# A convolution and SwiGLU kernel on one core: activation fetch in 1024-byte packets, eight sums on VectorE, the first output in column tiles, the last stores on two queues

## The chip, the cores and the metric

The kernel runs on one core of a Trainium2 chip. The metric is device time in microseconds of one execution. The engines are TensorE (PE; its weight loads are PEld), VectorE (DVE), ScalarE (ACT), GpSimd (POOL) and SyncE (SP), which issues most DMAs. ScalarE issues some.

## The reference

A causal convolution over time with 7 taps for each of 8 heads (taps are a softmax), then RMS norm and a feed-forward layer with SwiGLU. 8 x 4096 tokens of 192 features, 1536 hidden features, all in float32:

```python
w = softmax(weight, axis=-1)                       # 8 heads x 7 taps
attn = einsum('hk,bskhg->bshg', w, unfold(x))      # causal, 24 features a head
x = attn.reshape(32768, 192)
xn = x / sqrt(mean(x * x, axis=-1) + 1e-6) * rms_g
g, val = xn @ w_gate, xn @ w_val                   # 192 -> 1536
out = (g * sigmoid(g) * val) @ w_out               # 1536 -> 192
```

## The kernel before

The 32768 tokens are worked in 32 pairs of 1024 tokens (two groups g of 512). Gate and value weights stand side by side on the partitions: of each tile of 128 partitions the lower 64 rows belong to the gate, the upper 64 to the value, and a feature's 192 inputs are three slices k of 64 rows. So a product is six matmuls: three slices, each in two row halves that run beside each other.

**Pair 0** (`plain`, L1073) multiplies plainly. Its hidden values `ht` are multiplied with `wo_sb` in `outer` (L1098 on; matmuls L1114): 128 tokens as weights, 192 features as moving columns, the hidden features in two row halves. ScalarE copies the lower half's sums out of PSUM (L1122), VectorE adds the upper half's (L1126), and two stores of 384 KB go out (L1131).

**Pair 1** (word list `FIRST`) multiplies its products plainly too (L874), but its output already goes the way of all later pairs: `step` (L926) issues six matmuls that use 32 columns of the array each, with 32 features of the weights as stationary tile and 384, 256 or 128 columns of tokens. Between the products ten combinations of the weights are prepared for all later pairs. `prepare` splits each into three parts: a difference on GpSimd for some (L752), high bits on VectorE (L755), a scaled copy on ScalarE (L759), the rest on VectorE (L761), a difference on GpSimd (L765), a last copy on ScalarE (L767) and a store to DRAM (`wd`, L771). Two buffers take turns, so weight n waits until weight n - 2 is stored. The word `W` in the list is one such step.

**Pairs 2 to 31** (word list `ORDER`, once in each window `w`) use seven-product schemes on both levels: the products (L902) take split operands, float32 in three parts, from a ring of ten slots that is loaded from `wd` (L788); sums of hidden values (`h_sum`, L953) and of output accumulators (L970, L1000) make good for the products saved. `split` (L670, L816, L818) and `x_sum` (L830) make the operands' parts for the next pair while the present one runs.

The words name the engine, the act and the chunk: `Gh1.0` is h sum 1 of chunk 0 on GpSimd, `Vh1.0` the same on VectorE; `Aga.0` a silu on ScalarE (L976), `Vma.0` the product of silu and value (L983), which frees a PSUM bank; `p1` the next product or step on PE; `+` and `-` point to the next pair and the one before. A word's place in the list is its place in its engine's own order, and nothing else: each engine works its instructions in that order and waits where an operand isn't there.

A pair's activations are convolved in a layout of their own, stored to DRAM (`xd`, L1036, 192 rows of 4096 bytes), and fetched with features on the partitions in six transfers of 64 rows (`fetch`, L634). The tile that takes them is `xb`, for pair 2 `lent`, which lies where the ring will be. The first cast of a window (`An.0`, L670 on ScalarE) waits for the fetch of one slice. The next pairs' inputs are loaded by `load_head` (L149).

A pair's output is transposed on VectorE in blocks of 32 (`turn`, L941) and leaves in five stores for each of the two groups (`leave`, L1025). `leave` chooses the queue: `q = nc.scalar if c > 0 and p == PAIRS - 1 else queue(eng)`.

Of the kernel before, what the change touches and what calls it, by code (L numbers as in the profile page):

```python
# [20 lines left out]
def kernel(  # L21
# [10 lines left out]
    nc = tc.nc  # L32
# [34 lines left out]
    NP = FC // 2  # L67
    SPAN = 1509
# [168 lines left out]
    lent = spc.tile([P, 2 * KP * T], F32, name="ring")  # L237
# [107 lines left out]
    rb = cst.tile([P, KP, 2, T], F32, name="xb")  # L345
    lent4 = lent[:].rearrange("p (k g t) -> p k g t", k=KP, g=2)
# [3 lines left out]
    xb = rb[:].rearrange("p k g t -> p g k t")  # L350
# [297 lines left out]

    def pick(h, full):

        i = next((i for i in free[h] if ((h, i) in whole) == full), free[h][0])
        free[h].remove(i)
        return i

# [149 lines left out]

    def operand(g, p):
        if g < KP:
            return tokens(p)[:, g]
        return tt[:, 0:2, :] if g == 3 else tt[:, 2:4, :]

    def split(act, g, eng, p):  # L810
        src, high = operand(g, p), split_of(g, 0)
        e = engine.get(eng)
        if act == "n":
            copy(eng, high.bitcast(F32R), src)
        elif act == "l":
            e.tensor_tensor(out=split_of(g, 1).bitcast(F32R), in0=src, in1=high, op=ALU.subtract)  # L816
        else:
            nc.vector.scalar_tensor_tensor(  # L818
                out=split_of(g, 2).bitcast(F32R), in0=high, scalar=1.0 + SPLIT, in1=src,
                op0=ALU.mult, op1=ALU.subtract,  # L820
            )

    def x_sum(i, eng, p):
        a11, a21, a12, a22, e1, e2 = (tokens(p)[:, k // 2, k % 2] for k in range(6))
        s1, s2, s4, s3 = (tt[:, k, :] for k in range(4))
# [8 lines left out]
    class Pair:  # L834
        def __init__(self, p):
            self.p = p
            self.bk, self.o_sb, self.sg = {}, {}, {}
            self.open_half = {}
            self.line = self.products()
# [27 lines left out]
        def products(self):  # L867
            if self.p == 1:
                for j, c in PLAIN:
                    g, f = CELL[c]  # L870
                    self.open((j, c), False)
                    for k in range(KP):
                        for h in range(2):
                            nc.tensor.matmul(  # L874
                                out=self.both(j, c)[:, h, :], lhsT=wf[HALF[h], k, 2 * j + f, :],
                                rhs=rb[HALF[h], k, g, :], start=(k == 0), stop=(k == KP - 1),
# [33 lines left out]
        def step(self, form, k):  # L910
# [5 lines left out]
            right = RIGHT[form][:, k]  # L916
            two = src.rearrange("p (b q e) -> p q b e", q=2, e=Q)
            for i in range(2):
                self.tile(b, i, 0, WIDE, right[:, i], src[:, 0:WIDE], fresh)
            for i in range(2):  # L920
                self.tile(b, 2 + i, 0, T // 2, right[:, 2], two[:, i], fresh)
            for i in range(2):
                self.tile(b, 2 + i, T // 2, T - WIDE, right[:, i], src[:, WIDE:T], False)
# [31 lines left out]
        def do(self, eng, name):  # L955
# [47 lines left out]
            elif act in ("T22", "T21"):  # L1003
                self.turn(tt[:, 7 if act == "T22" else 8, :], 1, int(act[2]) - 1)
            elif act in ("T11", "T12"):
# [3 lines left out]
            else:  # L1009
                self.leave(int(act[2]), j, eng)  # L1010

        def leave(self, g, i, eng):
# [11 lines left out]
            q = nc.scalar if c > 0 and p == PAIRS - 1 else queue(eng)  # L1024
            q.dma_start(out=to, in_=o[i * Q : i * Q + n, lo:hi, :])  # L1025
# [75 lines left out]
    LAG = 138  # L1101

    STEP = 100 * D / T
    OUT = 2 * (T // P) * FC * STEP
    OVER = 50

    def outer(p, hts, base):


        def mm(h, bks, g, j, w, f, first, give=None):  # L1110
            if first:
                bks[h] = free[h].pop(0) if first is True else pick(h, False)
                whole.discard((h, bks[h]))
            nc.tensor.matmul(  # L1114
                out=bank(h, bks[h])[:, w : w + D],
                lhsT=hts[f // NF][HALF[h], g, f % NF, j * P : (j + 1) * P],
                rhs=wo_sb[HALF[h], f, :], start=(f == 0 and w == 0),
                stop=(f == FC - 1), skip_group_check=True,
            )

        def low(dst, bks, n):
            nc.scalar.copy(out=dst, in_=bank(0, bks[0])[:, 0:n])  # L1122
            free[0].append(bks[0])

        def upp(dst, bks, n):
            nc.vector.tensor_tensor(out=dst, in0=bank(1, bks[1])[:, 0:n], in1=dst, op=ALU.add)  # L1126
            free[1].append(bks[1])

        def store(g, o_sb, lo=0, hi=T // P):
            r = p * PT + g * T  # L1130
            nc.sync.dma_start(  # L1131
                out=out[r + lo * P : r + hi * P, :].rearrange("(j p) d -> p j d", p=P),
                in_=o_sb[:, lo:hi, :],
            )

        def soon(*a):
            put(base + n * STEP + LAG + OVER + 1, functools.partial(store, *a))

        n = 0

        def mms(bks, g, j, w, fs, first):
            nonlocal n
            for i, f in enumerate(fs):
                for h in range(2):
                    at = base + n * STEP + h * LAG
                    put(at, functools.partial(mm, h, bks, g, j, w, f, first if i == 0 else False))
                n += 1

        def evac(dst, bks, w):
            put(base + n * STEP + OVER, functools.partial(low, dst, bks, w))  # L1150
            put(base + n * STEP + LAG + OVER, functools.partial(upp, dst, bks, w))

        for g in range(2):
            o_sb = outs.tile([P, T // P, D], F32, name="o_sb")
            if g == 0:

                bks = [{}, {}]
                for fs in (range(0, FC // 2), range(FC // 2, FC - NF)):
                    for j in range(4):
                        mms(bks[j // 2], g, j, j % 2 * D, fs, j % 2 == 0 and fs[0] == 0)  # L1160
                for j in range(4):
                    mms(bks[j // 2], g, j, j % 2 * D, range(FC - NF, FC), False)
                    if j % 2:
                        dst = o_sb[:, j - 1 : j + 1, :].rearrange("p j d -> p (j d)")
                        evac(dst, bks[j // 2], 2 * D)
            else:
                for j in range(0, 2 if p == PAIRS - 1 else 4, 2):
                    b = {}
                    mms(b, g, j, 0, range(FC), "used" if j else True)
                    mms(b, g, j + 1, D, range(FC), False)  # L1170
                    evac(o_sb[:, j : j + 2, :].rearrange("p j d -> p (j d)"), b, 2 * D)

                if p == PAIRS - 1:
                    soon(g, o_sb, 0, 2)
                    for j in range(2, 4):
                        b = {}
                        mms(b, g, j, 0, range(FC), True)
                        evac(o_sb[:, j, :], b, D)
                        soon(g, o_sb, j, j + 1)
                    continue  # L1180
            soon(g, o_sb)
# [74 lines left out]
    put(base - 1, lambda: outer(0, first_hts, base))  # L1256
# [70 lines left out]
```

## Time and profile before

| | us |
|---|---|
| median of 3 runs | 2559.19 (2558.7 to 2560.28) |
| profiled execution | 2559.58 |
| its span | 2557.8 |
| PE busy, in the span | 2496.4 |

By stretches of the profiled execution (us; busy time of each engine, granted clock of PE):

| stretch | what | PE | DVE | ACT | POOL | PE clock | DMA busy |
|---|---|---|---|---|---|---|---|
| 92.77 to 129.17 | output of pair 0 | 33.73 | 15.40 | 6.05 | 21.45 | 1.00 | 0.34 |
| 129.17 to 198.03 | products of pair 1, weights prepared | 63.37 | 44.38 | 30.45 | 45.06 | 1.00 | 0.70 |
| 198.03 to 234.60 | output of pair 1, splits for pair 2 | 29.18 | 24.85 | 5.86 | 8.60 | 0.91 | 0.24 |
| 234.60 to 2549.10 | pairs 2 to 31 | 2284.12 | 1949.00 | 886.50 | 870.57 | 1.00 | 0.70 |
| 2549.10 to the end | last stores | 0.00 | 0.65 | 0.00 | 0.00 | | 0.41 |

The 30 windows from 234.60 on last 76.8 to 78.0 us each, counted from one window's first L902 record to the next. A row of the timeline gives start, duration, engine, line, operation, what it writes and reads, and in brackets the idle time before it and what ended that. A float32 matmul leaves two records; a matmul of L902, whose operands are of the type fp32r, leaves one. Of DMAs the trace holds issue times (the engine's name with a q) and a record for every packet with its size and duration.

### The profile page before, as it was taken

Reading aid. Unit: us, or ns where it says so; the run is one execution under the profiler, and the core shown is the slowest. Engines: PE = TensorE matmul, PEld = TensorE weight load, DVE = VectorE, ACT = ScalarE, POOL = GpSimd, SP = SyncE. Lnnn points to the kernel's source line nnn. Section 1 sums busy time; section 2 is a strip of 40 time slices with the busy share of each in tenths; the row PEclk is TensorE's granted clock in tenths of the full one; section 3 lists DMA queues with packets and bytes.
Section 4 is the critical chain, followed back from the end, with each engine's and each line's share of the span. In section 5 each row is a group of like instructions: output and inputs, shape, how many; then the busy total and the mean of one; then the engine's idle time right before and its main releaser. Section 6 shows DMA issues by size and latency. Waiting matters only on the chain.

```text
span 2557.8 us, 69178 instructions
## 1 busy us (share of the span) xinstructions
PE 2496.4 (98%) x28960; PEld 1921.2 (75%) x28960; DVE 2114.0 (83%) x2511; ACT 989.8 (39%) x1409; POOL 957.6 (37%) x671
## 2 busy tenths in 40 slices
PE   8998999999999999999999999999999999999998
PEld 5736777777777877777777777777777777777776
DVE  8667888889888898888888888898888898888874
ACT  6442343333343433343333343333343333443432
POOL 0462433333434333434333433333433334433332
PEclk9999999999999999999999999999999999999999
DMA  6364687666787666786667787666786666786652
GB/s 146 58 211 110 163 202 180 184 162 165 166 205 179 180 159 165 171 208 174 178 160 166 172 198 186 169 165 162 183 205 176 161 170 161 190 196 177 162 154 79
DMA packets 716105, 432.10 MB, mean 169 GB/s; under 512 B 508050, under 2 KB 702098, under 8 KB 715794
## 3 DMA queue, kind: packets, MB, share of 16 engines
q1 hardware_dynamic: 654944, 412.75, 64.9%
q10 hardware_dynamic: 60850, 14.92, 2.7%
q8 instruction: 229, 3.75, 0.6%
q14 instruction: 82, 0.67, 0.1%
HBM read 366.96 MB, written 60.56 MB: 167 GB/s over the span
## 4 chain that ended last, share of the span: by engine, by line
PE 86%; DVE 5%; DMA 3%; ACT 2%; issue 2%; POOL 1%; SPq 1%; ACTq 0%; DVEq 0%; POOLq 0%
PE ps L902 54%; PE ps L926 31%; ACT tt L976 1%; DVE ht L983 1%; DMA ring<-wd 1%; PE ps L1114 1%; DMA wd<-part 1%; DVE y L438 1%; DVE part L816 1%; DMA ht<-in_moe_w_gate_dram 0%; DVE ht L953 0%; POOL part L765 0%; SPq L232 0%; DVE ht L1091 0%; DMA xb<-xd 0%
## 5 line engine op out<-in xcount | busy, mean ns | idle before, releaser
L902 PE MATMUL ps<-part,ring 64*128 64x512 f32 x12240 | 1453.1, 391 | 12.7 <-issue 1.1
L902 PEld LDWEIGHTS ps<-part,ring 64*128 64x128 f32 x12240 | 1171.8, 184 | 280.1 <-issue 58.6
L976 ACT ACTIVATE tt<-ps 128x512 f32<-128x512 f32 x744 | 435.3, 599 | 979.5 <-PE ps L902 882.8
L983 DVE TENSOR_TENSOR ht<-ps,tt 128x512 f32<-128x512 f32 x744 | 503.0, 686 | 214.7 <-ACT tt L976 210.8
L926 PE MATMUL ps<-ht,x 128*32 128x384 f32 (+2 forms) x6696 | 410.3, 381 | 22.9 <-DVE ht L983 15.4
L953 POOL TENSOR_TENSOR ht<-ht 128x512 f32<-128x512 f32 x186 | 284.8, 1544 | 356.5 <-PE ps L926 263.2
L926 PE MATMUL ps<-ht,wo_sb 128*32 128x256 f32 (+2 forms) x6696 | 414.8, 380 | 2.2 <-ACT ps L670 1.9
L926 PEld LDWEIGHTS ps<-ht,x 128*32 128x32 f32 x6696 | 291.4, 110 | 118.2 <-issue 17.8
L970 DVE TENSOR_TENSOR ps<-ps,tt 128x1024 f32<-128x1024 f32 x240 | 295.7, 1232 | 100.9 <-PE ps L902 51.3
L926 PEld LDWEIGHTS ps<-ht,wo_sb 128*32 128x32 f32 x6696 | 288.3, 110 | 107.7 <-issue 12.1
L438 DVE SCALAR_TENSOR_TENSOR y<-xh,tp,y 128x1536 f32<-128x1536 f32 x186 | 354.3, 1905 | 1.2
L670 ACT COPY tt<-ps 128x384 f32<-128x384 f32 (+1 forms) x182 | 151.9, 835 | 245.7 <-PE ps L926 177.3
L953 POOL TENSOR_TENSOR hs<-ht 128x512 f32<-128x512 f32 x124 | 158.7, 1293 | 220.5 <-DVE ht L983 220.5
L467 POOL TENSOR_SCALAR r<-r 128x8 f32<-128x8 f32 x31 | 6.1, 197 | 582.1 <-DVE r L462 582.1
L816 POOL TENSOR_TENSOR part<-xb,part 128x1024 fp32r<-128x1024 f32 x58 | 169.6, 2925 | 49.1 <-ACT part L670 49.1
L953 DVE TENSOR_TENSOR ht<-hs,ht 128x512 f32<-128x512 f32 x155 | 166.2, 1089 | 5.4 <-DVE ht L953 0.5
L670 ACT COPY ps<-ps 128x384 f32<-128x384 f32 (+1 forms) x121 | 104.8, 867 | 121.7 <-DVE ht L983 93.8
L926 PE MATMUL ps<-hs,x 128*32 128x384 f32 (+2 forms) x2232 | 138.2, 379 | 0.0
L670 ACT CAST part<-xb 128x1024 fp32r<-128x1024 f32 x87 | 88.4, 1051 | 109.2 <-DMA xb<-xd 109.2
L818 DVE SCALAR_TENSOR_TENSOR part<-part,xb 128x1024 fp32r<-128x1024 f32 x87 | 130.7, 1502 | 0.0
L953 DVE TENSOR_TENSOR ht<-ht 128x512 f32<-128x512 f32 x186 | 124.3, 694 | 7.2 <-PE ps L926 6.0
L926 PEld LDWEIGHTS ps<-hs,x 128*32 128x32 f32 x2232 | 94.4, 110 | 33.5
(135 smaller groups left out, 1518.1 us busy)
## 6 DMA issues: line engine op xcount, KB each, us to landing
ring<-wd SPq DMA_DIRECT2D x1440, 192.0 KB
xb<-xd SPq DMA_DIRECT2D x180, 256.0 KB
xd<-xh SPq DMA_DIRECT2D x240, 96.0 KB
xh<-in_x_dram SPq DMA_DIRECT2D x192, 105.0 KB
wd<-part SPq DMA_DIRECT2D x9, 1152.0 KB
out_dram<-o_sb ACTq DMA_DIRECT2D x94, 96.0 KB
xh<-in_x_dram SPq DMA_DIRECT2D x56, 98.4 KB
out_dram<-o_sb ACTq DMA_DIRECT2D x32, 128.0 KB
```

The source lines that it names most:

```text
L438: nc.vector.scalar_tensor_tensor(out=y, in0=xk, scalar=w, in1=y, op0=ALU.mult, op1=ALU.add)
L467: nc.gpsimd.tensor_scalar(out=r, in0=r, scalar1=s / D, scalar2=s * 1e-6, op0=ALU.mult, op1=ALU.add)
L670: nc.scalar.copy(out=dst, in_=src)
L816: e.tensor_tensor(out=split_of(g, 1).bitcast(F32R), in0=src, in1=high, op=ALU.subtract)
L818: nc.vector.scalar_tensor_tensor(out=split_of(g, 2).bitcast(F32R), in0=high, scalar=1.0 + SPLIT, in1=src, op0=ALU.mult, op1=ALU.subtract,)
L902: nc.tensor.matmul(out=self.both(j, c)[:, h, :], lhsT=left[HALF[h]], rhs=right[HALF[h]], start=(first and q == 0), stop=True, skip_group_c ...
L926: nc.tensor.matmul(out=self.acc(b)[i * Q : (i + 1) * Q, at : at + n], lhsT=left, rhs=cols, start=fresh, stop=True, skip_group_check=True, ...
L953: engine[eng].tensor_tensor(out=dst, in0=a, in1=b, op=op)
L970: nc.vector.tensor_tensor(out=self.both(j, c), in0=self.both(j, "b"), in1=s5, op=ALU.add)
L976: nc.scalar.activation(out=tt[:, t, :], in_=self.both(j, c)[:, 0, :], func=AF.Silu)
L983: nc.vector.tensor_tensor(out=self.hv(j, "abcd".index(c)), in0=self.both(j, c)[:, 1, :], in1=tt[:, t, :], op=ALU.mult,)
L1114: nc.tensor.matmul(out=bank(h, bks[h])[:, w : w + D], lhsT=hts[f // NF][HALF[h], g, f % NF, j * P : (j + 1) * P], rhs=wo_sb[HALF[h], f, :] ...
```

## The change

There are four parts. (1) The tiles that take fetched activations get rows of four pieces of 256 elements with 2 elements between, so that a transfer's row of 4096 bytes becomes four packets of 1024; all that reads them takes four pieces. (2) In `FIRST` the eight h sums that GpSimd did (`Gh1.0` to `Gh3.4`) go to VectorE, and the loads `Sld` stand later in the list, with their place among SyncE's instructions as it was. (3) `outer` is replaced: pair 0's output takes the tiles of `step`, in four cells of one group and one half of the features, with transposes and ten stores in place of copies, additions and two stores; two groups of taps of pair 2's convolution are placed to fit. (4) The last pair's ten stores issue once all transposes of their group are done, group 1 first, the larger ones first, by turns on ScalarE's and SyncE's queue.

```diff
+    CUT = 4
+    GAP = PT // CUT + 2
...
-        "Vmc.0 W p1 Gpow+ W W W p1 W p1 Agd.0 W Vmd.0 p1 Vbc+ Gh1.0 p1 Gmul+ p1 Aga.1 Gh3.0 W",
+        "Vmc.0 W p1 Gpow+ W W W p1 W p1 Agd.0 W Vmd.0 p1 Vbc+ Vh1.0 p1 Gmul+ p1 Aga.1 Vh3.0 W",
...
-    lent = spc.tile([P, 2 * KP * T], F32, name="ring")
+    lent = spc.tile([P, KP * CUT * GAP], F32, name="ring")
...
-    rb = cst.tile([P, KP, 2, T], F32, name="xb")
-    lent4 = lent[:].rearrange("p (k g t) -> p k g t", k=KP, g=2)
+    rb = cst.tile([P, KP * CUT * GAP], F32, name="xb")
+    xb = rb[:, 0 : KP * PT].rearrange("p (k g t) -> p g k t", k=KP, g=2)
+
+    def pieces_in(t):
+        t = t[:, 0 : KP * CUT * GAP].rearrange("p (k c t) -> p k c t", k=KP, c=CUT)
+        return t[:, :, :, 0 : PT // CUT]
+
+    rb, lent4 = pieces_in(rb), pieces_in(lent)
...
             out=tokens(p)[rows, k],
-            in_=scr[p][k * HP : (k + 1) * HP, :].rearrange("p (g t) -> p g t", t=T),
+            in_=scr[p][k * HP : (k + 1) * HP, :].rearrange("p (c t) -> p c t", c=CUT),
...
+    def cut(t):
+        return t.rearrange("p g (c t) -> p (g c) t", t=PT // CUT)
...
-        src, high = operand(g, p), split_of(g, 0)
+        src, high, low, mix = operand(g, p), *(cut(split_of(g, i)) for i in range(3))
...
-                                rhs=rb[HALF[h], k, g, :], start=(k == 0), stop=(k == KP - 1),
+                                rhs=rb[HALF[h], k, g * CUT // 2 : (g + 1) * CUT // 2],
+                                start=(k == 0), stop=(k == KP - 1),
...
+            self.tiles(b, [right[:, m] for m in range(NM)], src, fresh)
+
+        def tiles(self, b, right, src, fresh):
...
+        def at_end(self, g):
+            self.turned[g] += 1
+            if self.p == PAIRS - 1 and self.turned[g] == 2:
+                for i in (2, 3, 1, 4, 0):
+                    self.leave(g, i, "AS"[i % 2])
...
-            q = nc.scalar if c > 0 and p == PAIRS - 1 else queue(eng)
-            q.dma_start(out=to, in_=o[i * Q : i * Q + n, lo:hi, :])
+            queue(eng).dma_start(out=to, in_=o[i * Q : i * Q + n, lo:hi, :])
...
+    STEP = 63
+
+    def outer(hts, base):
+
+        pair = Pair(0)
+        cells = [(1, 0), (1, 1), (0, 0), (0, 1)]
+
+        def mm(n, f):
+            g, i = cells[n]
+            if f == 0:
+                pair.bk[n] = free[0].pop(0)
+                whole.discard((0, pair.bk[n]))
+            right = wo_sb[:, f, :].rearrange("p (m n e) -> p n m e", n=2, e=Q)[:, i]
+            src = hts[f // NF][:, g, f % NF, :]
+            pair.tiles(n, [right[:, m] for m in range(NM)], src, f == 0)
+
+        def turn(n):
+            g, i = cells[n]
+            pair.turn(pair.acc(n), g, i)
+            free[0].append(pair.bk.pop(n))
+            if i == 1:
+                for c in range(5):
+                    pair.leave(g, c, "S")
+
+        for n in range(len(cells)):
+            for f in range(FC):
+                put(base + (n * FC + f) * STEP, functools.partial(mm, n, f))
+            put(base + (n + 1) * FC * STEP + 10, functools.partial(turn, n))
...
-        put(base + (1420 if k < 3 else 2100) + k, functools.partial(tap_of, 2, k, "V"))
+        put(base + (780 if k < 3 else 1540) + k, functools.partial(tap_of, 2, k, "V"))
```

More of the change, by code (lines that the diff above doesn't have):

```diff
@@ L647 @@
     whole = {(h, i) for h in range(2) for i in range(4)}
[L649 to L653, printed above, removed]
     line = []
@@ L823, in x_sum @@
     def x_sum(i, eng, p):
-        a11, a21, a12, a22, e1, e2 = (tokens(p)[:, k // 2, k % 2] for k in range(6))
-        s1, s2, s4, s3 = (tt[:, k, :] for k in range(4))
+        n = CUT // 2
+        a11, a21, a12, a22 = (
+            tokens(p)[:, k // 2, k % 2 * n : (k % 2 + 1) * n] for k in range(4)
+        )
+        s1, s2, s4, s3 = (cut(tt[:, k : k + 1, :]) for k in range(4))
         dst, a, b, op = {
@@ L916, in step @@
             right = RIGHT[form][:, k]
+            self.tiles(b, [right[:, m] for m in range(NM)], src, fresh)
+        def tiles(self, b, right, src, fresh):
             two = src.rearrange("p (b q e) -> p q b e", q=2, e=Q)
             for i in range(2):
-                self.tile(b, i, 0, WIDE, right[:, i], src[:, 0:WIDE], fresh)
+                self.tile(b, i, 0, WIDE, right[i], src[:, 0:WIDE], fresh)
             for i in range(2):
-                self.tile(b, 2 + i, 0, T // 2, right[:, 2], two[:, i], fresh)
+                self.tile(b, 2 + i, 0, T // 2, right[2], two[:, i], fresh)
             for i in range(2):
-                self.tile(b, 2 + i, T // 2, T - WIDE, right[:, i], src[:, WIDE:T], False)
+                self.tile(b, 2 + i, T // 2, T - WIDE, right[i], src[:, WIDE:T], False)
         def tile(self, b, i, at, n, left, cols, fresh):
@@ L1008, in do @@
                 self.give(b, 2)
-            else:
+                self.at_end(0)
+            elif p < PAIRS - 1:
                 self.leave(int(act[2]), j, eng)
+        def at_end(self, g):
[3 more added lines that the diff above has]
+                    self.leave(g, i, "AS"[i % 2])
         def leave(self, g, i, eng):
@@ L1099, in plain @@
         return products(), silus(), values()
[L1101 to L1181, printed above, removed]
```

12 lines of the change are left out of this document (6 added, 6 removed), and 20 rows, old and new, of the table FIRST.

## The prediction

> **What bounds the kernel now.** I read the head of the page first, then busy time in five stretches, then what TensorE (PE) waited for in them, then the timeline of the two stretches in which it waited most, and of the end.
>
> ```profile
> span 2557.8 us, 69178 instructions
> PE 2496.4 (98%) x28960; PEld 1921.2 (75%) x28960; DVE 2114.0 (83%) x2511; ACT 989.8 (39%) x1409; POOL 957.6 (37%) x671
> ```
>
> PE is busy for 98% of the span, so the 30 windows from 234.6 to 2549.1 us leave little: 2284.12 busy us in 2314.50. What PE waited for there:
>
> ```profile
> PE ps L926 <- DVE ht L983: 15.4, 28, 0.6
> PE ps L926 <- ACT ps L670: 1.9, 5, 0.4
> PE ps L902 <- DMA ring<-wd: 1.1, 2, 0.9
> ```
>
> (Columns: us in total, times, longest.) The first row is one short wait in each window, PE to silu to VectorE and back to PE; no part of the change shortens that chain. Ahead of 234.6 stands more, in pair 0's output (L1114) and pair 1:
>
> ```profile
> 92.77 14.46 PE L1114 MATMUL ps<-wo_sb,ht 64*128 64x192 f32 x168
> 107.49 2.22 PE L1114 MATMUL ps<-wo_sb,ht 64*128 64x192 f32 x24 [0.26 <-ACT o_sb L1122]
> 110.27 8.07 PE L1114 MATMUL ps<-wo_sb,ht 64*128 64x192 f32 x96 [0.56 <-ACT o_sb L1122]
> 118.91 8.06 PE L1114 MATMUL ps<-wo_sb,ht 64*128 64x192 f32 x92 [0.56 <-ACT o_sb L1122]
> 129.17 31.40 PE L874 MATMUL ps<-xb,part 64*128 64x512 f32 x144 [0.72 <-DVE o_sb L1126]
> ```
>
> ```profile
> PE ps L926 <- DVE ht L953: 7.4, 1, 7.4
> PE ps L874 <- DVE ht L983: 5.5, 4, 2.1
> ```
>
> (The second fence is PE's waits from 129 to 234 us.) The last four output tiles and the first product each waited for an eviction. In pair 1 the L874 products lost 5.5 us in four waits, and the output steps 7.4 us in one.
>
> **Part 1, first output in column tiles.** Removed: 192 matmuls of L1114 (384 records, an f32 matmul leaves two) from 92.77 to 129.17, 36.4 us with their waits, and four ScalarE copies (0.48) and four VectorE additions (0.56). Added: 4 cells of 12 steps of six matmuls, the shape of L926 with `wo_sb` as weights:
>
> ```profile
> 220.19 4.08 PE L926 MATMUL ps<-ht,x 128*32 128x384 f32 x72
> 224.06 1.51 PE L926 MATMUL ps<-hs,x 128*32 128x384 f32 x24
> ```
>
> 72 records are six steps, and the next group starts 3.87 us on: 0.645 a step, 48 steps 31.0 us. To this comes the change between row halves and column tiles: in a later window 48 records of L926 take 2.74 us to the next L902 record, not 4 x 0.645 = 2.58, so 0.16 each way, 0.3. And one wait: the new order takes f = 0 to 11 in the first cell, f = 10 at 92.77 + 6.45 = 99.2, while GpSimd's last piece of `wo_sb` (L330) ends at 100.27: 1.1 us. The four cells take four banks, and pair 1's first product takes the bank of the first cell, long read, so the 0.72 goes. Products start at 92.77 + 31.0 + 0.3 + 1.1 = 125.2: **-4.0 us**. The eight transposes (0.65 a cell, L941) lie beside PE. On SyncE ten stores take the place of two; the last five wait for the last transpose (near 126) and issue for some 3 us, and behind them stands the first prepared weight, ready at about 135.
>
> **Part 2, h sums of pair 1 on VectorE.** What holds the L874 products is not PE: their evictions (L983) queue on VectorE behind the preparation of the ten weights (L755, L761, then L765 on GpSimd), and that waits for one of two buffers to be stored. GpSimd's share:
>
> ```profile
> 144.66 1.59 POOL L953 TENSOR_TENSOR hs<-ht 128x512 f32<-128x512 f32 x1
> 146.21 2.85 POOL L488 TENSOR_TENSOR xh<-y,s 128x1536 f32<-128x1536 f32 x1
> 146.34 3.47 DVE L761 SCALAR_TENSOR_TENSOR part<-part 128x768 f32<-128x768 f32 x1 [1.23 <-ACT part L759]
> 148.96 1.98 POOL L953 TENSOR_TENSOR ht<-ht 128x512 f32<-128x512 f32 x1
> 150.90 2.12 POOL L765 TENSOR_TENSOR part<-part 128x768 f32<-128x768 f32 x1
> ```
>
> L761 takes 0.96 us alone and here 3.47, ending 0.75 after L488: it stands while GpSimd works. The eight sums that move cost GpSimd 11.4 us and VectorE 0.69 each, 5.5 us, up to 1.8 each beside a GpSimd operation. VectorE is busy for 44.38 of 68.86 us in this stretch, so they fit if they stand ahead of nothing urgent. From a start 4.0 earlier, weight 1's L765 ends at 140.7, L488 runs to 144.5 with its own start at 141.6, L761 of weight 2 ends 0.75 later and L765 starts at 145.3, where it was 150.90: -5.6. Weights 4 and 6 follow at 10.2 to 10.5 us (stores at 153.92, 164.38 and 174.50 now), so weight 7 is ready some 6 us earlier, near 174.
>
> Then comes a queue: the fetch of pair 2's activations (five issues of 256 KB) stands ahead of weight 7's store. Now its packets run from 179.37 to 184.86 and the store's to 187.96, and the L755 of weight 9 starts at 188.62. After the change the fetch begins near 173.5 and lasts 3.9 to 5.5, the store 3.5, so L755 starts at 181.9 to 183.2. The products end 9.5 us behind it (198.09 now), so at 192.0: **-6.0 with part 1**, of which 2.0 are part 2's. What follows (7.4 us of wait, VectorE's splits and sums) hangs on that end and moves with it.
>
> **Part 3, 1024-byte fetch.** The packet records give 306 ns for a 4096-byte packet (159 for those right after idle), 65 for most of 1536 bytes, 36 for most of 768. No 1024-byte packet moves now. Bounds: 40 (a quarter of 159) and 98 (the slow tenth of those of 1536); 76 would be the same rate as now. The row near in shape (3072 bytes into 64 partitions, 220) says no gain, the rows near in size say 46 to 50. I take 50, since 3840 bytes into 112 partitions are as slow (259). The first four fetches, which free the first cast of a window (L670), are 16 packets on each engine: 16 x (306 - 200) = 1.7 us earlier. Most windows gain nothing: they last 77.0 us where the cast starts by 48.8 us from the window's first product. Nine cast later (49.0 to 50.3), and last 3.5 us more in all: **-3.5**, at worst nothing. That wait:
>
> ```profile
> ACT part L670 <- DMA xb<-xd: 109.2, 29, 5.6
> ```
>
> Operands in four pieces of 256 keep their element count; L438 reads 64 x 24 at the same 0.85 elements per ns as L818 a flat 1024, so nothing.
>
> [...]
>
> **Part 4, last stores.**
>
> ```profile
> 2549.12 0.65 DVE L941 STREAM_TRANSPOSE o_sb<-ps 128x256 f32<-128x256 f32 x2 [2.28 <-PE ps L926]
> 2549.80 4.97 ACTq L1025 DMA_DIRECT2D out_dram<-o_sb  x9
> ```
>
> Nine stores issue on ScalarE's queue, 0.55 each, all behind the last transpose; the last issues at 2554.15 and lands 2.5 us on. After: half g = 1 goes out at 2546.9, when its own transposes end; after 2549.8 remain three on ScalarE and two on SyncE, the last issued at 2550.9, landed at 2553.4: **-3.2**. 1536 packets of 256 bytes at 20 ns on 16 engines are 1.9 us, inside that. ScalarE has no other work there.
>
> **Sum.** -6.0 - 3.5 - 3.2 = -12.7. The profiled execution took 2559.58 (span 2557.8), 0.39 over the median of the three, 2559.19. 2559.58 - 12.7 = 2546.9, and 2546.5 against that median.
>
> **Rivals.**
> - Part 2 is given back and the fetch is hidden: the sums on VectorE meet GpSimd's operations, as L953 on VectorE does (0.69 alone, 1089 ns mean where it reads `hs`), and eight times 0.5 to 1 us eat the 2.0. For it: they stand in order ahead of L755. -4.0 - 3.2: **2552**. Chance 0.2.
> - Four packets cost more than one: most packets of 96 bytes take 12 ns and of 256 bytes 18, so 8.4 ns stand beside the bytes, and three packets more add 25 ns to 306. The first four fetches get 16 x 25 ns = 0.4 us longer, some 16 windows cast past 48.8 and lose about 0.2 each: -6.0 - 3.2 + 3 gives **2553**. [...] Chance 0.1.
> - Slower: pieces that start 8 bytes further each time take 100 ns. The cast comes 16 x 4 x 24 ns = 1.5 us later, at 49.9. The latest now, at 50.34, made its window 78.02, 1.0 more for 1.5 past 48.8, so 0.7 x 29 windows = +21, and -9.2 beside it: **2571**. It decides from 92 ns a piece. [...] Chance 0.07.
> - More: with earlier splits the 7.4 us wait shrinks below what halves the clock (it was granted 0.5 from 212.4 to 219.2), 4 us more: **2542**. Chance 0.08.
> - That a part does nothing: the stores may be bound by their bytes. Then 2 us less gain, inside the range.
>
> **How the numbers follow.** Forecast 0.55 (2543 to 2550), the rest as above. The range 2541 to 2554 takes in all but the slow case and the tails. 0.2% (5.1 us) is about what a measurement of this kernel can tell from no change; faster by more than that is below 2554.1: forecast, first and fourth rival, most of the second: 0.88. Within: 0.05. Slower: 0.07.
>
> **What would show it.** First product of pair 1 near 125; last of them near 192; L765 of weight 2 near 145; first cast of a window 1 to 2 us earlier and no window over 77.3; the last issue within 1.3 us of the last transpose. I am wrong if the windows' mean moves by over 0.2 us either way, or if pair 1's products wait as long as now.

## The result, and the profile after

| | before | after |
|---|---|---|
| median of 5 runs, us | 2559.19 (2558.7 to 2560.52) | 2550.81 (2547.83 to 2551.6) |
| profiled execution, its span | 2559.58, 2557.8 | 2551.32, 2549.5 |

The changed kernel takes 0.9964 of the time [0.995, 0.9979], 8.4 us less; 2546.5 was forecast. The head of the page of the changed kernel:

```profile
span 2549.5 us, 69568 instructions
PE 2496.1 (98%) x29152; PEld 1920.8 (75%) x29152; DVE 2106.9 (83%) x2523; ACT 988.3 (39%) x1405; POOL 929.1 (36%) x663
```

PE's busy time hardly moved (2496.4 before), though one stretch shrank by 4.05 us: something else made PE's work longer. To find it I cut both spans at the same events:

| stretch | before | after | change | forecast |
|---|---|---|---|---|
| span's start to pair 0's first output step | 92.77 | 93.40 | +0.6 | 0 |
| from there to window 2 (the front) | 141.83 | 139.80 | -2.0 | -6.0 |
| the next 29 windows | 2237.53 | 2234.24 | -3.3 | -3.5 |
| last window and last stores | 85.66 | 82.09 | -3.6 | -3.2 |

(The first row is the same code in both kernels; in the fourteen kernels of this study it was 91.8 to 93.4, so the rows below are counted from pair 0's first output step.) In size two terms came out as forecast and one did not. The timeline of PE in the front, changed kernel (start, duration, engine, line, what it writes and reads, records, and in brackets the wait before it; L936 was L926, L880 was L874, L993 was L983, L963 was L953):

```profile
93.40 6.71 PE L936 MATMUL ps<-ht,wo_sb 128*32 128x384 f32 x120
100.91 24.91 PE L936 MATMUL ps<-ht,wo_sb 128*32 128x384 f32 x456 [0.80 <-POOL wo_sb L332]
125.75 31.17 PE L880 MATMUL ps<-xb,part 64*128 64x512 f32 x144
157.63 13.15 PE L880 MATMUL ps<-xb,part 64*128 64x512 f32 x60 [0.71 <-DVE ht L993]
171.73 5.42 PE L880 MATMUL ps<-xb,part 64*128 64x512 f32 x24 [0.96 <-DVE ht L993]
177.98 2.85 PE L880 MATMUL ps<-xb,part 64*128 64x512 f32 x12 [0.83 <-DVE ht L993]
181.14 2.85 PE L880 MATMUL ps<-xb,part 64*128 64x512 f32 x12 [0.31 <-DVE ht L993]
187.22 9.69 PE L880 MATMUL ps<-xb,part 64*128 64x512 f32 x36 [3.23 <-DVE ht L993]
196.84 3.46 PE L936 MATMUL ps<-ht,wo_sb 128*32 128x384 f32 x60
...
213.35 4.07 PE L936 MATMUL ps<-ht,x 128*32 128x384 f32 x36 [5.91 <-DVE ht L963]
```

The last wait of the products and the wait behind them, before:

```profile
190.10 8.00 PE L874 MATMUL ps<-xb,part 64*128 64x512 f32 x36 [2.14 <-DVE ht L983]
198.03 3.46 PE L926 MATMUL ps<-ht,wo_sb 128*32 128x384 f32 x60
...
216.02 3.71 PE L926 MATMUL ps<-ht,x 128*32 128x384 f32 x36 [7.39 <-DVE ht L953]
```

The first three rows of the changed kernel are part 1 as forecast: 32.35 us from the first output step to the first product, where 32.4 was written down and 36.40 stood before. The products then begin 4.05 earlier and end only 1.8 earlier. Their waits sum to 6.0 us, 5.5 before: those ahead of the last shrank in sum from 3.4 to 2.8, the last grew from 2.14 to 3.23. The 36 records behind it take 9.69 us, where the same 36 took 8.00 before. The same stretches with the clock (columns: us, busy us of PE, weight loads, DVE, ACT and POOL, the granted clock, DMA's share and rate):

```profile
157.63:187.22 29.59, 24.26 (x109) 9.96 (x109) 16.96 (x24) 11.82 (x19) 12.99 (x8) 1.00 0.89 273
187.22:196.84 9.62, 9.62 (x37) 3.98 (x37) 7.71 (x9) 4.82 (x7) 7.04 (x5) 0.82 0.85 141
196.84:213.35 16.51, 10.61 (x194) 8.04 (x192) 14.67 (x17) 3.43 (x5) 3.08 (x3) 0.97 0.10 29
213.35:233.20 19.85, 19.85 (x312) 14.62 (x312) 7.10 (x9) 2.43 (x3) 2.36 (x2) 0.85 0.26 82
```

and the last three of them before:

```profile
190.10:198.03 7.93, 7.93 (x37) 3.40 (x37) 5.36 (x8) 4.82 (x7) 5.63 (x5) 1.00 0.93 197
198.03:216.02 17.99, 10.61 (x194) 8.04 (x193) 17.84 (x18) 3.43 (x5) 6.25 (x4) 0.90 0.21 40
216.02:234.60 18.58, 18.58 (x312) 13.74 (x312) 7.00 (x9) 2.43 (x3) 2.35 (x2) 0.91 0.26 86
```

Behind the 3.23 us wait the clock was granted at 0.5 from 188.40 for 3.41 us: 1.7 us of new PE time. Behind the 5.91 us wait it is halved as before (212.29 to 219.12), but PE resumes earlier in that stretch, so its steps need 19.85 us where they needed 18.58. PE's chain of waits names what the last product waited for:

```profile
174.46 0.85 ACT part L767
...
175.33 10.31 DMA wd<-part
...
185.74 0.31 DVE part L755
```

and before:

```profile
180.04 8.48 DMA wd<-part
```

(Start, duration, what.) The store of weight 7 is issued at 175.33 and lands 10.31 us later; before it took 8.48. The fetch of pair 2 stands ahead of it, and its packets now run from 174.66 to 180.78, 6.1 us, where they took 5.5.

The windows have gained, but not by earlier casts (us of wait in total, times, longest):

```profile
ACT part L670 <- DMA xb<-xd: 130.1, 29, 5.7
```

The casts wait 0.7 us longer in each window (109.2 in total before). The end of the program, with six issues on ScalarE's queue and four on SyncE's in two groups:

```profile
2542.00 5.08 ACTq L1042 DMA_DIRECT2D out_dram<-o_sb  x6
2542.20 3.71 SPq L1042 DMA_DIRECT2D out_dram<-o_sb  x4
2544.45 0.65 DVE L951 STREAM_TRANSPOSE o_sb<-ps 128x256 f32<-128x256 f32 x2 [2.28 <-PE ps L936]
```

The last issue starts at 2546.28, 1.2 us behind the last transpose, where it was 4.35. That this row of the table is part 4's shows in all kernels of this study: from the last window's start to the end of the span it is 82.0 to 82.4 us in the nine profiles with part 4, and 85.4 to 85.7 in the five without.

### The profile page after: what moved, and what is told of

Same layout as the page of the kernel before. It is cut to its first block, busy times and chain, and to the rows that moved or that the text cites. A ratio compares the mean times of both kernels' runs of the same rounds, so it can differ in the third digit from the quotient of the medians.

```text
span 2549.5 us, 69568 instructions
## 1 busy us (share of the span) xinstructions
PE 2496.1 (98%) x29152; PEld 1920.8 (75%) x29152; DVE 2106.9 (83%) x2523; ACT 988.3 (39%) x1405; POOL 929.1 (36%) x663
## 4 chain that ended last, share of the span: by engine, by line
PE 84%; DVE 5%; DMA 5%; ACT 2%; issue 2%; SPq 1%; POOL 1%; DVEq 0%; ACTq 0%; POOLq 0%
PE ps L909 52%; PE ps L936 32%; DMA xb<-xd 2%; DVE ht L993 1%; ACT tt L986 1%; DMA ring<-wd 1%; DMA wd<-part 1%; DVE y L445 1%; SPq L641 0%; DVE part L819 0%; DMA ht<-in_moe_w_gate_dram 0%; DVE ht L963 0%; DVE ht L1108 0%; SPq L151 0%; PE ps L880 0%
## 5 line engine op out<-in xcount | busy, mean ns | idle before, releaser
L993 DVE TENSOR_TENSOR ht<-ps,tt 128x512 f32<-128x512 f32 x744 | 502.6, 686 | 212.9 <-ACT tt L986 206.7
L936 PE MATMUL ps<-ht,wo_sb 128*32 128x384 f32 (+2 forms) x7272 | 450.1, 381 | 2.4 <-ACT ps L670 1.5
L936 PE MATMUL ps<-ht,x 128*32 128x256 f32 (+2 forms) x6696 | 414.1, 381 | 19.2 <-DVE ht L993 13.1
L963 POOL TENSOR_TENSOR ht<-ht 128x512 f32<-128x512 f32 x182 | 276.1, 1530 | 362.2 <-PE ps L936 271.5
L936 PEld LDWEIGHTS ps<-ht,wo_sb 128*32 128x32 f32 x7272 | 320.8, 110 | 112.8 <-issue 14.0
L936 PEld LDWEIGHTS ps<-ht,x 128*32 128x32 f32 x6696 | 295.5, 110 | 112.7 <-issue 17.4
L445 DVE SCALAR_TENSOR_TENSOR y<-xh,tp,y 128x1536 f32<-128x1536 f32 x186 | 348.8, 1875 | 1.4 <-issue 0.2
L963 POOL TENSOR_TENSOR hs<-ht 128x512 f32<-128x512 f32 x120 | 153.2, 1289 | 220.4 <-DVE ht L993 220.4
L819 POOL TENSOR_TENSOR part<-xb,part 128x1024 fp32r<-128x1024 f32 x58 | 159.5, 2750 | 46.7 <-ACT part L670 46.7
L963 DVE TENSOR_TENSOR ht<-hs,ht 128x512 f32<-128x512 f32 x155 | 158.9, 1041 | 5.2 <-PE ps L909 0.5
L936 PE MATMUL ps<-hs,x 128*32 128x384 f32 (+2 forms) x2232 | 139.8, 379 | 0.0
L963 DVE TENSOR_TENSOR ht<-ht 128x512 f32<-128x512 f32 x190 | 128.4, 698 | 8.4 <-PE ps L936 7.0
L821 DVE SCALAR_TENSOR_TENSOR part<-part,xb 128x1024 fp32r<-128x1024 f32 x87 | 127.7, 1468 | 0.0
L936 PEld LDWEIGHTS ps<-hs,x 128*32 128x32 f32 x2232 | 99.9, 110 | 29.7
## 6 DMA issues: line engine op xcount, KB each, us to landing
ring<-wd SPq DMA_DIRECT2D x1440, 192.0 KB
```

What stands on the lines that cost most here:

```text
L445: nc.vector.scalar_tensor_tensor(out=y, in0=xk, scalar=w, in1=y, op0=ALU.mult, op1=ALU.add)
L819: e.tensor_tensor(out=low.bitcast(F32R), in0=src, in1=high, op=ALU.subtract)
L821: nc.vector.scalar_tensor_tensor(out=mix.bitcast(F32R), in0=high, scalar=1.0 + SPLIT, in1=src, op0=ALU.mult, op1=ALU.subtract,)
L936: nc.tensor.matmul(out=self.acc(b)[i * Q : (i + 1) * Q, at : at + n], lhsT=left, rhs=cols, start=fresh, stop=True, skip_group_check=True, ...
L993: nc.vector.tensor_tensor(out=self.hv(j, "abcd".index(c)), in0=self.both(j, c)[:, 1, :], in1=tt[:, t, :], op=ALU.mult,)
```

## The experiments

Twelve kernels, in three groups (e, f and g), each group on a chip of its own with the kernel before beside it. The times of one kernel spread by 2 to 7 us, and in the profiles a few windows of each execution are longer than the rest; what a part does in the front is read from the profile. All kernels, in us from pair 0's first output step:

| kernel | median of runs | first product | weight 7's store issued | L755 of weight 9 | products' end | window 2 | median window |
|---|---|---|---|---|---|---|---|
| before | 2559.19 | 36.40 | 87.27 | 95.85 | 105.26 | 141.83 | 77.02 |
| after | 2550.81 | 32.35 | 81.93 | 92.34 | 103.44 | 139.80 | 76.89 |
| e1, whole rows | 2551.82 | 32.40 | 82.20 | 91.83 | 102.94 | 139.35 | 77.04 |
| e2, sums on GpSimd | 2550.64 | 32.39 | 83.74 | 94.22 | 105.32 | 141.55 | 76.88 |
| e3, fetch behind the store | 2551.8 | 32.38 | 81.96 | 87.87 | 99.32 | 140.54 | 76.89 |
| e4, rows shifted | 2552.0 | 32.34 | 81.93 | 91.80 | 102.91 | 138.81 | 77.06 |
| f1, fetch spread | 2544.03 | 32.34 | 82.87 | 88.37 | 99.01 | 135.41 | 76.86 |
| f2, two pieces | 2549.85 | 32.37 | 82.05 | 91.92 | 103.02 | 138.92 | 76.87 |
| f3, sums alone | 2556.24 | 36.40 | 85.70 | 94.27 | 103.68 | 139.90 | 77.02 |
| f4, outer alone | 2556.42 | 32.35 | 83.70 | 93.46 | 104.57 | 140.62 | 77.02 |
| g1, spread, wait filled | 2540.36 | 32.36 | 82.83 | 88.38 | 99.02 | 132.57 | 76.87 |
| g2, outer and spread | 2552.44 | 32.38 | 84.49 | 89.69 | 100.36 | 136.78 | 77.00 |
| g3, before and spread | 2556.12 | 36.40 | 88.25 | 92.93 | 103.68 | 139.68 | 77.01 |
| g4, g1 in two pieces | 2542.49 | 32.36 | 82.84 | 88.34 | 98.98 | 132.53 | 76.89 |

### e1: whole rows again

```diff
-    GAP = PT // CUT + 2
+    GAP = PT // CUT
```

> The changed kernel, but the four pieces of a row lie without a gap, so a fetch writes whole rows of 4096 bytes again and part 3 is undone. Theory A (the fetch in small packets is slower, 356 ns against 306 for a row, and what part 3 gained came from operations on the gapped rows): first casts of the windows 0.7 us earlier than in the changed kernel, yet GpSimd's L819 back from 2.75 to 2.92 us and the usual window back from 76.82 to 77.00; pair 2's fetch 0.9 us shorter (5.4 for 6.3), weight 9's L755 1 to 2 us earlier than 185.74, products of pair 1 end at 193.5 to 195.5. Windows +3.3, front -1.5 to -3.5: 2550 to 2553 us. Rival B (the smaller packets gained the windows): casts later, windows +3.3 or more, front unchanged: 2554 or more.

2551.82 us (2548.92 to 2552.86), 0.9965 of before [0.9951, 0.9978]: no different from the changed kernel. Both halves of theory A show in the rows of the profile: the 29 windows take 1.9 us more and the front 0.45 less, and the start, the same code, 0.9 less. The fetch's packets are of 4096 bytes again (301 ns each in the mean, against four of 1024 at 89, 356 together), and the casts wait 108.7 us in all for them. The front gains less than the 1.5 to 3.5 expected: weight 9 starts only 0.5 us earlier, and a last wait of 2.61 us still halves the clock. Two of GpSimd's groups with `xb` as an operand, between 400 and 2400 us, in the changed kernel (L819 was L816 before, L836 was L830):

```profile
L819 POOL TENSOR_TENSOR part<-xb,part 128x1024 fp32r<-128x1024 f32 x52 | 142.5, 2741 | 41.5 <-ACT part L670 41.5
L836 POOL TENSOR_TENSOR tt<-tt,xb 128x512 f32<-128x512 f32 x26 | 40.9, 1573 | 91.1 <-DVE tt L836 87.9 <-DMA xh<-in_x_dram 3.2
```

and with whole rows:

```profile
L819 POOL TENSOR_TENSOR part<-xb,part 128x1024 fp32r<-128x1024 f32 x52 | 151.2, 2908 | 43.9 <-ACT part L670 43.9
L836 POOL TENSOR_TENSOR tt<-tt,xb 128x512 f32<-128x512 f32 x26 | 43.3, 1666 | 88.6 <-DVE tt L836 75.1 <-DMA xh<-in_x_dram 13.5
```

(The number behind the busy time is the mean in ns.) The same operations are 6% quicker where a row lies in pieces with a gap. Rival B is out: the casts came earlier with whole rows, not later.

### e2: the sums back on GpSimd

Of the word list, the changed words alone:

```diff
-Vh1.0 Vh3.0 Vh1.1 Vh3.1 Vh1.2 Vh1.3 Vh3.3 Vh3.4
+Gh1.0 Gh3.0 Gh1.1 Gh3.1 Gh1.2 Gh1.3 Gh3.3 Gh3.4
```

> The changed kernel with the eight h sums of pair 1 back on GpSimd (part 2 undone). Theory A (the fetch ahead of weight 7's store and the TensorE clock, halved from 188.40 for 3.41 us after a wait of 3.2, hold the products' end; the sums do little): weight 7's store issues at 176.0 (180.04 less the 4.0 of part 1; 175.33 in the changed kernel), L755 of weight 9 10.4 us later, products end within 1 us of 196.84: 2550 to 2553 us. Rival C (the sums on VectorE themselves hold up pair 1's products): products end at 194.0 (198.03 less 4.0), 2.8 us earlier, 2547.5 us. The forecast on record would have them end 2 us later, 2553.

2550.64 us (2549.73 to 2556.97). The front answers: products' end 1.9 us later than in the changed kernel and window 2 1.75 later. The median did not follow; in the profiled executions the 29 windows took 2.4 us less than in the changed kernel (2231.85 for 2234.24) and the start 1.3 less, both the same code. Rival C, that the sums hold up the products, is out: they are worth 1.8 us, about the 2.0 forecast for them. Theory A was wrong that they do little: without them parts 1 and 3 together gain 0.3 us of front.

### e3: the fetch behind weight 7's store

```diff
-"Sft.0+ p1 Sft.1+ Agc.3 Sft.2+ Vmc.3 p1 Sft.3+ W p1 Sft.4+ W W W Sft.5+ p1 Agd.3 W",
+"p1 Agc.3 Vmc.3 p1 W p1 W W W Sft.0+ Sft.1+ Sft.2+ Sft.3+ Sft.4+ Sft.5+ p1 Agd.3 W",
```

> The changed kernel with pair 2's fetch issued behind weight 7's store instead of ahead of it (six words of the order moved; nothing else). Theory A (that queue holds weight 9, and the halved clock behind the wait takes 1.7 us more): the store issued at 175.3 lands near 180.3, L755 of weight 9 starts at 180.5 instead of 185.74, the last wait of the products falls under 1 us, no halved clock near 188, products end at 190 to 191.5 instead of 196.84; the casts of window 1's operands come no later than now (190.57), so window 2 starts 3 to 6 us earlier: 2545 to 2548 us. Rival D (what follows the products waits for the fetch, which now lands near 186, or for VectorE): products end near 190.5, but PE's wait before the last output steps of pair 1 grows by as much, 8 to 12 us instead of 5.9, and the time stays within 1.5 us of the changed kernel's.

2551.8 us (2549.22 to 2553.75): nothing gained, as rival D had it. PE in this kernel:

```profile
180.08 10.57 PE L880 MATMUL ps<-xb,part 64*128 64x512 f32 x48 [0.32 <-DVE ht L993]
191.92 3.46 PE L936 MATMUL ps<-ht,wo_sb 128*32 128x384 f32 x60 [1.27 <-DVE ht L993]
...
213.63 4.07 PE L936 MATMUL ps<-ht,x 128*32 128x384 f32 x36 [9.82 <-DVE ht L963]
```

The store did land early (L755 of weight 9 5.9 us behind its issue, 10.4 before the move), the long wait of the products and its halved clock went, and the products end 4.1 us earlier. But now the fetch and the last two stores come late, and the first cast of what pair 2 needs (on ScalarE) starts when the last of them lands:

```profile
192.19 1.99 ACT L670 CAST part<-ring 128x1024 fp32r<-128x1024 f32 x2 [8.62 <-DMA wd<-part]
```

The stall moved behind the products. By this run the order within the stretch is worth nothing: the fetch and the stores still have to pass in one stretch in which DMA is nearly always busy (0.89 above). f1 takes them apart.

### e4: rows shifted, not cut

```diff
+    PITCH = CUT * GAP
-t = t[:, 0 : KP * CUT * GAP].rearrange("p (k c t) -> p k c t", k=KP, c=CUT)
-return t[:, :, :, 0 : PT // CUT]
+t = t[:, 0 : KP * PITCH].rearrange("p (k t) -> p k t", k=KP)[:, :, 0:PT]
+return t.rearrange("p k (c t) -> p k c t", c=CUT)
```

> The changed kernel with whole rows of 4096 bytes (as e1) at a pitch of 4128 bytes instead of 4096 (4 x 1032, the room that the changed kernel takes). Tells the shift of the rows from the gaps inside a row. If it is the rows' addresses that made GpSimd's operations on the activations quicker: L819 2.75 us, usual window 76.82, casts as early as in e1, 2546 to 2549 us. If it is the four pieces of an operand: L819 2.92, windows 77.00, the same time as e1.

2552.0 us (2550.33 to 2553.75). GpSimd's subtraction takes 2959 ns and the median window 77.06: it is the pieces, not the addresses of the rows.

### f1: the fetch spread

```diff
-... p1 W W W p1 W p1 Agc.2 ...
+... p1 W W Sft.0+ Sft.1+ W p1 W p1 Agc.2 ...
-"Vmd.2 p1 W W W Vh1.2 ... p1 Agb.3 W W W Vmb.3 ...
+"Vmd.2 p1 W W Sft.2+ Sft.3+ W Vh1.2 ... p1 Agb.3 W W Sft.4+ Sft.5+ W Vmb.3 ...
-"Sft.0+ p1 Sft.1+ Agc.3 Sft.2+ Vmc.3 p1 Sft.3+ W p1 Sft.4+ W W W Sft.5+ p1 Agd.3 W",
+"p1 Agc.3 Vmc.3 p1 W p1 W W W p1 Agd.3 W",
```

> The changed kernel with pair 2's fetch issued earlier, two of its six pieces behind each of the stores of weights 4, 5 and 6 (159.8, 164.9 and 169.8 us), where the DMA engines idle some 1.7 us of every 5. Theory E (the first cast of a window's operands, 190.57, waits for the last weight's store, and that for the DMA engines, which move 6.1 MB without a break from 170.5 to 188; some 22.8 us of VectorE's work behind that cast set when the last output steps of pair 1 run, whatever the products do): the store issued at 175.3 lands near 180, L755 of weight 9 starts at 180.2, the last store lands near 185.5, the first cast starts 4 to 5 us earlier than in the changed kernel, no halved clock near 188, and from pair 0's first output step to window 2 it takes 4 to 6 us less than 139.80: 2545 to 2547 us. Rival D2 (VectorE's or GpSimd's own work sets the end): cast earlier, but what follows it longer than 22.8 by as much, time within 1.5 us of the changed kernel's.

2544.03 us (2541.68 to 2546.48), 0.9936 of before [0.9924, 0.9949]: 6.8 us less than the changed kernel and below the 2545 to 2547 expected. The front is 4.4 us shorter; the rest, in the profiles, lies in the windows and the start, which are the same code. No clock is halved near 188, and the last 48 products run through. Theory E held in what the queue takes (its 6.1 MB between 170.5 and 188 us are 5.1 by the packet records). Its other half, that 22.8 us behind the first cast set the end whatever the products do, fell: here they are 21.6. What stays the same is 16.5 us from the products' end to PE's next steps (in the changed kernel, e1, e2, e4, f1 and f2 alike); in e3 they are 21.7, because the fetch comes last there. In the kernel before they are 18.0 and VectorE is busy for 17.84 of them, in the changed kernel for 14.67: so before, VectorE's own work set the end, and in f3, g2 and g3 it nearly does (17.4 to 17.6 us, VectorE busy for 16.6 to 17.1).

### f2: two pieces of 512

```diff
-    CUT = 4
+    CUT = 2
```

> The changed kernel with a row in two pieces of 512 (2048-byte packets) instead of four of 256. If any cut of an operand makes GpSimd quicker: L819 2.74 us, usual window 76.85 to 76.9, casts 0.3 to 0.5 us earlier than with four pieces: 2549 to 2551 us. If it goes by the number of pieces: L819 near 2.83, usual window 76.95, 2551 to 2552 us. If neither, as e1: 2.91 and 77.04.

2549.85 us (2546.6 to 2552.55). The same two groups of GpSimd:

```profile
L819 POOL TENSOR_TENSOR part<-xb,part 128x1024 fp32r<-128x1024 f32 x52 | 141.2, 2716 | 43.2 <-ACT part L670 43.2
L836 POOL TENSOR_TENSOR tt<-tt,xb 128x512 f32<-128x512 f32 x26 | 43.5, 1672 | 89.8 <-DVE tt L836 76.3 <-DMA xh<-in_x_dram 13.5
```

L819 takes 2716 ns and the median window is 76.87: two pieces do it as well as four. L836 reads 512 elements, which lie in one piece here and in two in the changed kernel, and it is as slow as on whole rows. So it is the gap inside an operand that counts, and not the size of the packets that DMA writes meanwhile, which is the same for both groups. A 2048-byte packet takes 159 ns in the mean, 318 for a row.

### f3 and f4: the sums alone, the outer alone

f3 is the kernel before with the eight words of e2 turned from G to V. f4 is the changed kernel with e1's and e2's edits and the last stores as before.

> The kernel before with part 2 alone: the eight h sums of pair 1 on VectorE. Theory E: the weights come 0.5 to 1.5 us earlier, and the last store with them; from pair 0's first output step to window 2 1 to 2 us less than 141.83: 2557 to 2559 us. By the forecast on record (its part 2 alone): 2557.6. If the sums on VectorE only collide with GpSimd's work: no change, 2560.

> Part 1 alone: the changed kernel with the sums on GpSimd, whole rows of 4096 bytes and the last stores as before. By the forecast on record the products of pair 1 start and end 4.0 us earlier and all behind them moves along: 2556 us. Theory E: products start 4.0 us earlier, but the stores of the weights only 3.5, and what they gain is partly lost in the queue of DMAs and to a halved clock: from pair 0's first output step to window 2 0.5 to 1.5 us less than 141.83, windows as before: 2558.5 to 2559.5 us.

2556.24 us (2554.91 to 2557.13), 0.9984 [0.9976, 0.9993], and 2556.42 us (2554.42 to 2558.95), 0.9989 [0.9981, 0.9998]. In the front the sums alone gain 1.9 us, and part 1 alone 1.2 of its 4.05; both together (e1) 2.5. The medians gained 2.9 and 2.7 us against the 2559.09 beside them, more than the front; the intervals (1.8 to 6.1 and 0.5 to 4.9 us) hold both. So the time of part 1 alone came out as the forecast's 2556 and not as theory E's 2558.5 to 2559.5, while its front gained what theory E said; the rest would have to lie in the windows and the start, which are the same code. Part 1's row shows where its gain ends: the store of weight 7 comes 3.6 earlier, L755 of weight 9 2.4, products' end 0.7.

### g1: the wait filled

```diff
-... Vh4.3 p1 Gh4.2 p5
+... Vh4.3 p1 Gh4.2 p1 H p4
+            elif word == "H":
+                flat = wo_sb[:].rearrange("p f d -> p (f d)")
+                warm = Pair(0)
+                warm.bk["W"] = pool4[0]
+                for i in range(8):
+                    left = [flat[:, m * Q : (m + 1) * Q] for m in range(NM)]
+                    warm.tiles("W", left, flat[:, 0:T], i == 0)
```

> The kernel with the fetch spread, and in PE's wait ahead of the last output steps of pair 1 (201.4 to 207.4 us) eight steps of matmuls (48, some 5.2 us) on constant operands into a free bank of PSUM that nobody reads. Theory F (the clock is granted by cells of 3.413 us: one in which PE idles for more than about half halves the next): no halved clock from 206.3 to 213.2, the 26 steps behind the wait take 17 us instead of 19.87, 1.5 to 2.9 us less in all: 2541 to 2542.5 us. Rival (the matmuls come in the way of the steps behind them, or VectorE's sums hold these steps anyway): the stretch behind the wait stays within 0.5 us of 19.87 in sum with the wait, 2544 us.

2540.36 us (2539.92 to 2544.41), 0.9931 [0.9919, 0.9944], the quickest here. The wait and the steps behind it, without the filling (f1):

```profile
201.44:207.36 5.92, 0.00 (x1) 0.01 (x1) 5.82 (x9) 0.00 (x0) 0.52 (x1) 0.91 0.24 75
207.36:227.23 19.87, 19.87 (x313) 14.75 (x314) 7.09 (x9) 2.43 (x3) 2.35 (x2) 0.85 0.24 80
```

and with it:

```profile
201.91:208.09 6.18, 5.47 (x105) 3.68 (x95) 6.08 (x10) 0.00 (x0) 0.52 (x1) 1.00 0.24 70
208.09:225.12 17.03, 17.03 (x312) 12.71 (x312) 7.10 (x9) 2.44 (x3) 2.36 (x2) 1.00 0.29 94
```

The wait is about as long as it was, now with matmuls that serve nothing, the clock stays at 1.00, and the same 312 records behind it take 2.84 us less. That is what theory F expected of this wait.

### g2 and g3: is part 1's gain in the queue?

g2 is f4 with the fetch spread, g3 the kernel before with only the fetch spread.

> Part 1 alone with pair 2's fetch spread behind the stores of weights 4 to 6. Theory E (what the fetch in the queue takes, part 1 can't give): from pair 0's first output step to window 2 135 to 136.5 us, 2 to 3 us less than in the next kernel, where part 1 without the spread was worth 1.2: 2551.5 to 2553 us. Rival D2 (VectorE's work behind the first cast limits it): within 1.2 us of the next kernel.

> The kernel before with nothing changed but the place of pair 2's fetch, spread behind the stores of weights 4 to 6. Theory E: store of weight 7 issued at 180 lands near 184.6 instead of 188.5, from pair 0's first output step to window 2 137.5 to 138.5 us instead of 141.83: 2555 to 2556 us. Rival: VectorE's work sets the end, no change, 2559.

2552.44 us (2551.03 to 2555.18) and 2556.12 us (2553.76 to 2557.55). Beside the spread fetch part 1 is worth 2.9 us of front (139.68 to 136.78), where alone it was worth 1.2 (f4), and 3.7 us of time, where alone it was worth 2.7. That is theory E, and D2 as the whole limit is out. g3's own gain was smaller than expected (2.15 us of front, 3.3 to 4.3 expected): L755 of weight 9 comes 2.9 earlier, but PE, which at 182.64 still has 60 records to go, runs them without a wait and ends 10.75 us behind L755 instead of 9.41.

### g4: both, in two pieces

```diff
-    CUT = 4
+    CUT = 2
```

> The kernel with the fetch spread and the filled wait, and rows in two pieces of 512 instead of four of 256 (2048-byte packets). Expected as the kernel with the filled wait, less 0 to 1.5 us for casts that come earlier in the windows: 2540 to 2542 us.

2542.49 us (2541.11 to 2542.89), just over the range expected; the front is g1's to 0.04 us, and the windows took 2.2 us more in the profiled runs. Between the seven profiles with cut rows they differ by up to 3.8, so this says nothing of the packets: no gain from bigger ones is seen here.

## Why the prediction was right in sign and too large

The measured 2550.81 lies within the range, nearer the first rival's 2552 than the forecast's 2546.5. But that rival counted 4.0 us for part 1 and nothing for the windows, where the rows show 2.0 for the front and 3.3.

**Part 1** was right as far as it goes: 32.35 us to the first product (32.4 forecast), the `wo_sb` wait 0.80 (1.1). **Part 4** was right: -3.6 for -3.2, the last issue 1.2 us behind the last transpose.

**The step that failed is the products' end, "so at 192.0: -6.0 with part 1"**. Counted from the first output step it should have come at 99.2 and came at 103.4. One of the forecast's own signs of being wrong, that pair 1's products wait as long as now, came true: 6.0 us for 5.5. The 4.2 us, by the forecast's own steps:

- weight 7 ready "near 174": 0.7 late, counted from the first output step. L765 of weight 2 ran at 147.37, not 145.3 (1.4 late, counted so). The forecast put L761 behind GpSimd's L488 (L495 now) and let the sums pass; in fact L755 met it (2.64 us instead of 0.55 alone), the first two sums beside GpSimd took 1.93 and 2.18, and L495 3.34 instead of 2.85. That is the first rival's mechanism, but small: e2 and f3 still put the sums' worth at 1.8 and 1.9.
- fetch and store: L755 of weight 9 came 10.4 us behind the store's issue, 8 to 9 forecast (the lower end of its terms adds up to 181.6, not 181.9), so 1.9 late. The fetch took 6.1 us and not at most 5.5, because of part 3, which I had priced apart and as a gain; in e1, with whole rows, the lag is still 9.6. What the other microsecond is stays open: of the store's 768 packets nearly all have started by 184.4, it lands at 185.64, and the last packets of the fetch piece behind it end at 185.84 too; no run tells why these last ones come late.
- "the products end 9.5 us behind it": 11.1. The 1.6 is the halved clock, which the forecast weighed for the 7.4 us wait alone.

From there on "what follows moves with it" held but for 1.5 us more of gain (16.5 us to PE's next steps; 18.0 before, when VectorE's own work filled them). The steps then run longer at half clock (+1.3), so the front gained 2.0 in all. f4, f3 and e1 say the same without part 3: part 1 alone 1.2, the sums alone 1.9, both 2.5. f1 takes the fetch out of the queue and the front gains 6.4, g1 takes the clock out as well and it gains 9.3.

**Part 3: the term was right (-3.3 for -3.5) and every step of it wrong.** A 1024-byte packet takes 89 ns in the mean, not 50; four take 356 ns where one took 306, 16% more. The second rival had the direction and half the size (25 ns, 50 measured). The casts came 0.7 us later, not 1 to 2 earlier, and five windows passed 77.3. The gain came from a term put at nothing, "operands in four pieces of 256 keep their element count [...] so nothing". The rows it rested on, L438 and L818, are VectorE's, and none of GpSimd's stood beside them. GpSimd's operations on the pieces are 6% quicker, VectorE's that stand beside them too (L821, L818 before: the last of a window 1.44 us for 1.59), so the last sums and transposes of a window end earlier, and the first 24 products of the next, which wait for a transpose, take 2.87 us in the median instead of 3.02 (in one window of before that I followed, the 13th product waited for L941). The medians of the fourteen profiles do not overlap in this: 2.86 to 2.88 with cut rows, 3.01 to 3.05 without. Over the seven profiles with cut rows a window takes 77.005 us in the mean, over the seven without 77.128: 3.6 us in 29 windows, with the later casts already in it. That the total came near is luck: two errors of opposite sign.

The rival of the earlier wait below the clock's halving (2542) did not come in the changed kernel: the wait shrank to 5.91 and the clock was halved all the same, and once more behind the 3.23 us wait.

## What to carry to other kernels

When a start is moved forward, follow the gain through every shared queue up to the next place where all engines meet: here 4.05 us became 1.2, because stores and a fetch had to pass through the same busy stretch of DMA, and moving the fetch into gaps 3 to 10 us earlier gave 4.4 us of front on top of the change, more than parts 1 and 2 together (2.5); in the kernel before it gave 2.15. Swapping two transfers within a full stretch (e3) only moved the wait. And look at the granted clock behind the longer waits of PE: here it stayed full behind one of 2.14 us (before) and was halved behind one of 2.61 (e1), one of 3.23 us cost 1.7 more, and filling one of 5.9 with matmuls that nobody reads gave 2.84 back.

## What the runs showed of the hardware

**The clock changed on a grid of 3.413 us.** All halved stretches of these kernels begin on it (in the changed kernel 188.40 and 212.29 are seven cells apart, and the two stretches last 3.413 and 6.827 us). I took PE's idle share in every such cell that ran at full clock. In the fronts of the fourteen profiles no cell up to 0.49 idle is followed by a halved one, and all 18 from 0.62 on are (0.62 and 0.65 in e1 and the changed kernel, waits of 2.61 and 3.23 us); at the end of f1 a cell with 0.57 is followed by a full one. The 2.14 us wait of the kernel before fell into a cell with 0.47. Once halved, it stayed so more easily: halved cells with 0.28 idle or more (13) were followed by another, those with 0.16 or less by a full one. So the 5.91 us wait, which reaches 0.31 into the first halved cell, cost two. In the fourteen profiles the first stretch of full clock begins anywhere from 7.8 to 11.0 us behind the span's start (11.0 before, 10.9 in the changed kernel).

**GpSimd was quicker on an operand in pieces.** A subtraction of 128 x 1024 took 2908 to 2959 ns on rows in one piece and 2716 to 2741 on two or four pieces 8 bytes apart; shifting whole rows did nothing (e4, 2959), and an operand of 512 in one piece stayed slow in the kernel whose other operands were cut (f2, 1672 ns; 1573 in two pieces in the changed kernel). Why is open.

**Packets into 64 partitions**, in the mean of a profile: 298 to 306 ns for 4096 bytes, 159 to 160 for 2048, 86 to 89 for 1024.
